# Retention attention and two MLPs on one core: plain products between the first attention units, four staging tiles, and weights moved between queues

## The chip, the cores and the metric

The kernel runs on one core of one Trainium2 chip. The metric is the device time of one execution in microseconds (us); lower is better. Three runs of the kernel before took 1064.4, 1069.26 and 1070.01 us, so its median is 1069.26 us.

The engines are TensorE (PE; its weight loads are shown apart as PEld), VectorE (DVE), ScalarE (ACT) and GpSimd (POOL). SyncE (SP) does no arithmetic here: it issues DMA transfers, and so does POOL. Each engine works through its own instructions in order.

## The reference, cut to what matters

An attention with a decaying state feeds a first MLP, which feeds a second.

```python
# q, k, v: (4 batches, 8 heads, 768 positions, 64)
gamma = 1.0 - 2.0 ** (-5.0 - np.arange(H))
for t in range(S):
    state = gamma * state + outer(k[:, :, t], v[:, :, t])
    y[:, :, t] = scale * einsum('bhd,bhde->bhe', q[:, :, t], state)
x = y.transpose(0, 2, 1, 3).reshape(3072, 512)

h = x @ w_in                      # first MLP: 512 -> 2048 -> 512
x = np.maximum(0.01 * h, h) @ w_out
h = np.maximum(x @ w_in2, 0.0)    # second MLP, weights of its own
return h * h @ w_out2
```

## The kernel before, in words

**Tiles.** The 3072 tokens are worked on in three blocks of 1024, each of two tiles of 512 tokens. A layer's 2048 inner columns are cut into 8 pairs (`NQ = 8`, the `q` of the code), each of two groups of 128 columns in each half. Weights are cast on the chip: ACT and DVE turn a piece into a high part and a low part (`scale_words`, `shift`, `sign`, `add`, then `high` and `low`), and a product is made of high x high, high x low and low x high, so a product of 128 columns is twelve matmuls of 128x512.

**Attention.** It is cut into 24 units. `attend` issues one: 64x64 matmuls `sc`, `y` and `inc` on PE, mask and state steps on DVE, copies on ACT. A unit is at most 120 matmuls and as many weight loads. The inputs `r` (queries, keys, values) come by loads on SP, `prep_to` prepares them. Units 0 to 7 stand in the head of the program, the others between the products of layer one. Inside layer one, `group()` issues a unit and the loads for the next units.

**Layer one, block one.** `emit_plain(q, i, t)` is a plain product (twelve matmuls) of pair q; `put_out` and `emit_out` are the products with the output weights, which add into the banks `acc`. In the head two plain products stand behind units 5 and 6. `begin_loop` ends the head, `plain_period(q)` runs for q = 1 to 7, and a second half of steps i = 0 to 15 puts out the other half, with a `group()` at i = 0, 2, 4, 6 and 8. From q = 4 on a period has a group as well.

**Layer one, block two.** `strassen_period(q)`, q = 0 to 7, uses seven products in place of eight. In the same stretch further weights are cast: `load_piece(n)` reads a 512 KB piece of the raw weights (`st<-w`) into a staging tile, `begin` casts it on ACT and DVE. Two staging tiles alternate (`t{NQ - 2 + n % 2}`).

**Later blocks.** `both_block(lay, b)` runs four times, first (0,2), then (1,0), (1,1) and (1,2), each with nine steps n: the first half of pair n and the second half of pair n - 1. In (1,0) the sums of the output weights of the second MLP that are still missing are made beside it: `make_units(q, f, ...)` reads a half of the weights (`of<-wflt`, on the POOL queue, since it goes by `store`) and adds up and casts quarters of it. Input weights of a pair come by `wa<-wid` and `wb<-wid` on the SP queue.

**What sets the order.** In `strict` stretches (the head, the periods) every instruction keeps the order in which the code issues it; elsewhere a scheduler orders them on each engine by the data they need. `mm` (L133) records every matmul, `load` (L136) issues a transfer on SP and `store` (L139) one on POOL, so most rows of a profile carry one of these lines, and the names of the tiles tell which step it is.

Of the kernel before, what the change touches and what calls it, by code (L numbers as in the profile page):

```python
# [47 lines left out]
MORE = 12  # L48
SOON = [(q, 0) for q in FIRST + (0, 1, 4, 6)] + [(q, 1) for q in range(NQ) if q not in HERE]
# [7 lines left out]
def retention_then_two_mlps(  # L57
# [251 lines left out]
    wou = [dram.tile([P, 8, NQ, 2, 256], F32, name=f"wou{lay}") for lay in range(2)]  # L309
# [257 lines left out]
    def sums_low(q):  # L567

        f = quarters_of(stage.pop(("of", q)))
        for n, (t, u) in enumerate(stage.pop(("u", q))):  # L570
            low(u[:, :, 1], f[:, 2 * n:2 * n + 2], u[:, :, 0])
            store(
                out=wou[0][:, 4 + 2 * n:6 + 2 * n, q].rearrange("p n l c -> p n (l c)"),
                in_=t.rearrange("p (n c) -> p n c", n=2),
            )
# [21 lines left out]
    def sum_units(lay, q, f, *to):  # L597
        sum_up(f)
        for n in range(2):
            out_units(lay, q, 4 + 2 * n, f[:, n * 512:n * 512 + 512].rearrange("p (n c) -> p n c", n=2), to[n])  # L600

    def all_units(q, f, *to):
# [3 lines left out]
        sum_units(1, q, f, *to[2:])  # L606
# [220 lines left out]
    def read_stage(lay, n, ks):  # L827
        i = STAGES[n]
        for k in ks:
            if n < 5:  # L830
                tag = (("xh1", "xl1", "xh5", "xl5"), ("xh6", "xl6", "xh3", "xl3"), ("xh7", "xl7", "xh2", "xl2"))[n % 3 if n < 3 else n - 2][k]
                t = x_p.tile([P, 2, 2, 256], F32R, tag=tag, name="wu")
            else:
                t = g_p.tile([P, 2, 2, 256], F32R, tag=f"t{4 * (n - 5) + k}", name="wu")
            load(out=t.bitcast(F32), in_=wou[lay][:, OUNIT[i], 2 * k:2 * k + 2])
            units[i, k] = t
# [79 lines left out]
    def both_block(lay, b, here):  # L916

        nl, nb = (lay, b + 1) if b + 1 < NB else (1, 0) if not lay else (None, None)
        pa = None
        for n in range(NQ + 1):  # L920
            f = first_half(lay, b, n) if n < NQ else iter(())
            r = second_half(lay, b, n - 1, pa) if n else iter(())
            if (lay, b) == (1, 0) and 3 <= n <= 6:
                with aside():
                    next(here[n // 5], None)
            if (lay, b) == (1, 0) and n == NQ - 1:
                with aside():
                    next(made, None)
            for k in range(4):
                pa = next(f, None)  # L930
                if n == NQ - 1 and k < 2:
                    read_stage(lay, 0, (2 * k, 2 * k + 1))
                if lay == 0 and n and (k == 1 or k == 3 and n in (1, 2, 4, 5)):
                    with aside():
                        next(here, None)
                if k < 3:
                    next(r, None)
            if n == NQ - 1:
                read_stage(lay, 1, range(4))
            if n and n + 1 < NQ and ((lay, b) != (1, 0) or n not in (3, 5)):  # L940
                read_units(lay, n + 1)
            if (lay, b) == (1, 0) and n < NQ - 1 and n != 5:
                if n == 0:
                    v = quarters() + scratch("ss", "ss", "wb", "wf")
                else:
                    with aside():
                        next(made, None)
                if n in (0, 2, 4):
                    made = make_units(5 + n // 2, *v[:5])
                    next(made)  # L950
                    if n == 0:
                        here = [units_here(4, v[5], v[7]), units_here(6, v[6], v[5])]
                        for m in here:
                            next(m)
# [77 lines left out]
    loads_to(1)  # L1032
    load_w(0, 0)
    load(out=tabs_t, in_=tabs)
    loads_to(NP)
    prep_to(1)
    h = [slice(0, 512), slice(512, 1024)]
    for n in range(ND):
# [4 lines left out]
        if n == 0:  # L1043
            s, f = open_in(0)
            for c in h:
                scale_words(s[:, c], f[:, c])
        elif n == 1:
            a = hold_in(0)
            for k in range(2):
                high(a[:, 0, 2 * k:2 * k + 2], quarters_of(f)[:, 2 * k:2 * k + 2])  # L1050
        if n == 0:
            prep_to(2)
# [5 lines left out]
        elif n == 1:  # L1058
            for k in range(2):
                o = slice(2 * k, 2 * k + 2)  # L1060
                low(a[:, 1, o], quarters_of(f)[:, o], a[:, 0, o])
        elif n == 4:
            load_w(1, 0)
            load_w(0, 1)
        if n == 6:
            first_in = open_in(1)
            scale_words(*first_in)
        if n in (5, 6):
            emit_plain(0, n - 5, 0)
        if n == 6:  # L1070
            shift(first_in[1])
            sign(*first_in)
# [4 lines left out]
    add(*first_in)  # L1077
# [29 lines left out]
    def begin_loop(first):  # L1107

        (w, f), out = first
        load_w(2, 0)  # L1110
        load_w(1, 1)
        load_w(2, 1)
        a = hold_in(1)
        high(a[:, 0], quarters_of(f))
        emit_plain(0, 0, 1)
        low(a[:, 1], quarters_of(f), a[:, 0])
        store(out=wraw[1], in_=f)
        emit_plain(0, 1, 1)
# [5 lines left out]
        for j in range(2):  # L1124
            split_high(j)
            split_rest(j)

    def plain_period(q):

        last = q == NQ - 1  # L1130
        early = q > 1

        load_w(q + 2, 0)
        if early:
            split_high(2 * q - 2)
# [5 lines left out]
        if not early:  # L1141
            o = hold_out(0)
            high_out(0, o)
        emit_plain(q, 0, 0)
        if early:
            split_rest(2 * q - 2)
            sums_high(q - 1)
        else:
            low_out(0, o)
# [4 lines left out]
        if early:  # L1154
            split_high(2 * q - 1)
        emit_plain(q, 1, 0)
        if early:
            split_rest(2 * q - 1)
            sums_low(q - 1)
# [18 lines left out]
        if not early:  # L1178
# [3 lines left out]
        for s, r in out:  # L1182
            add(s, r)
        if not early:
            sum_up(stage["of", 0])
        load_w(q + 2, 1)

        put_out(0, 2 * q - 2)
        if early and not last:
            a = hold_in(q + 1)  # L1190
            high(a[:, 0], quarters_of(f))
            low(a[:, 1], quarters_of(f), a[:, 0])
        if last:
# [3 lines left out]
        if not early:  # L1197
            sums_high(0)
        if q == 2:
            loads_to(ND + 1)  # L1200
            value_loads_to(ND + 1)
            loads_to(ND + 2)
        if q > 3:
# [5 lines left out]
        if not early:  # L1209
            sums_low(0)  # L1210
        if not last:
            sum_up(stage["of", q])
        if q >= 3:
            prep_to(n_score[0] + 1)
# [9 lines left out]
    def strassen_period(q):  # L1224
# [41 lines left out]
        load_piece(n + 1)  # L1266
# [13 lines left out]
        load_piece(n + 2)  # L1280
# [64 lines left out]
    for b in range(NB - 1):  # L1345
        strict[0] = True
        if b == 0:
            begin_loop((first_in, out0))
            for q in range(1, NQ):
# [25 lines left out]
        for i in range(NJ):  # L1375
# [6 lines left out]
            if b == 0 and i in (0, 2, 4, 6, 8):  # L1382
# [101 lines left out]
```

## Time and profile before

| | |
|---|---|
| median of three runs | 1069.26 us |
| the profiled execution, own time | 1072.81 us |
| its span, first to last instruction | 1071.0 us |
| PE busy | 1031.1 us (96%) |
| DVE busy | 763.6 us (71%) |
| ACT busy | 584.6 us (55%) |
| granted clock of PE, mean | 0.988 |
| moved by DMA | 294.01 MB, mean 275 GB/s |

The profiled execution lies 3.6 us above the median; 1.8 us of its time lie outside its span. PE is the engine to look at: where it stands still, the table of waits says what it waited for. The granted clock is a share of full speed (2.4 GHz); 0.50 is the lower of its two levels, 1.2 GHz. "issue" as a cause of a wait means that the engine waited for nothing that the profile shows.

### The profile page before, as it was taken

Reading aid. Unit: us, or ns where it says so; the run is one execution under the profiler, and the core shown is the slowest. Engines: PE = TensorE matmul, PEld = TensorE weight load, DVE = VectorE, ACT = ScalarE, POOL = GpSimd, SP = SyncE. Lnnn points to the kernel's source line nnn. Section 1 sums busy time; section 2 is a strip of 40 time slices with the busy share of each in tenths; the row PEclk is TensorE's granted clock in tenths of the full one; section 3 lists DMA queues with packets and bytes.
Section 4 is the critical chain, followed back from the end, with each engine's and each line's share of the span. In section 5 each row is a group of like instructions: output and inputs, shape, how many; then the busy total and the mean of one; then the engine's idle time right before and its main releaser. Section 6 shows DMA issues by size and latency. Waiting matters only on the chain.

```text
span 1071.0 us, 18364 instructions
## 1 busy us (share of the span) xinstructions
PE 1031.1 (96%) x7135; PEld 843.8 (79%) x7135; DVE 763.6 (71%) x1272; ACT 584.6 (55%) x996; POOL 91.6 (9%) x156
## 2 busy tenths in 40 slices
PE   5899999799898999999999998999999999999998
PEld 4678888687787788887788777888888888888886
DVE  5688878686687759487888767977555868356953
ACT  3566655445546447377566556655455555455542
POOL 0012111101000000122110111100000001000000
PEclk9999999999999999999999998999999999999999
DMA  8489967997999978889987487977256775367461
GB/s 306 164 326 376 325 254 236 404 329 260 361 389 342 357 251 296 331 308 393 355 286 314 155 306 273 404 254 287 86 200 223 298 270 201 128 206 258 171 239 59
DMA packets 81445, 294.01 MB, mean 275 GB/s; under 512 B 8400, under 2 KB 8656, under 8 KB 74704
## 3 DMA queue, kind: packets, MB, share of 16 engines
q1 hardware_dynamic: 61536, 212.56, 55.1%
q0 software_dynamic: 19680, 80.23, 19.2%
q8 instruction: 56, 0.92, 0.3%
q14 instruction: 29, 0.24, 0.1%
q10 hardware_dynamic: 144, 0.07, 0.0%
HBM read 206.84 MB, written 85.98 MB: 273 GB/s over the span
## 4 chain that ended last, share of the span: by engine, by line
PE 78%; DMA 14%; DVE 3%; ACT 2%; issue 2%; SPq 0%; POOL 0%; ACTq 0%; DVEq 0%; POOLq 0%
PE acc L133 42%; PE pa L133 21%; PE pd L133 8%; DMA st<-w 6%; DMA r<-first 4%; PE pb L133 4%; DMA of<-wflt 2%; PE y L133 2%; PE inc L133 1%; DMA wa<-wid 1%; PE sc L133 1%; DMA wraw<-wf 1%; SPq L136 0%; DMA wid<-wa 0%; ACT gh L732 0%
## 5 line engine op out<-in xcount | busy, mean ns | idle before, releaser
L133 PE MATMUL acc<-rot,wu 128*128 128x512 f32 x1344 | 308.3, 391 | 0.0
L133 PEld LDWEIGHTS acc<-rot,wu 128*128 128x128 f32 x1344 | 252.4, 188 | 55.3
L133 PE MATMUL pa<-xh,wa 128*128 128x512 f32 x576 | 179.9, 394 | 3.3 <-ACT g L721 1.4
L841 DVE TENSOR_TENSOR rot<-gu,rot 128x512 fp32r<-128x512 f32 x160 | 109.4, 689 | 46.4 <-ACT rot L840 45.5
L840 ACT CAST rot<-gu 128x512 fp32r<-128x512 f32 x160 | 99.4, 621 | 77.2 <-PE acc L133 53.6
L133 PEld LDWEIGHTS pa<-xh,wa 128*128 128x128 f32 x576 | 107.7, 189 | 29.1 <-DMA wa<-wid 3.0
L133 PE MATMUL acc<-gh,wo 128*128 128x512 f32 x400 | 106.0, 398 | 7.0 <-ACT gh L732 7.0
L133 PE MATMUL pa<-xl,wa 128*128 128x512 f32 x288 | 112.7, 391 | 0.0
L133 PE MATMUL pd<-xh,wa 128*128 128x512 f32 x320 | 99.7, 393 | 2.7 <-ACT gt L862 2.7
L133 PE MATMUL pa<-xh,wb 128*128 128x512 f32 x320 | 100.3, 395 | 0.5 <-DVE gt L875 0.5
L133 PEld LDWEIGHTS acc<-gh,wo 128*128 128x128 f32 x400 | 75.2, 190 | 24.9 <-ACT gh L732 8.3
L133 PEld LDWEIGHTS pd<-xh,wa 128*128 128x128 f32 x320 | 60.4, 189 | 15.8 <-ACT gt L862 3.1
L133 PEld LDWEIGHTS pa<-xh,wb 128*128 128x128 f32 x320 | 59.6, 189 | 14.0 <-DVE gt L875 1.4
L841 DVE TENSOR_TENSOR rot<-gt,rot 128x512 fp32r<-128x512 f32 x64 | 44.1, 691 | 29.4 <-ACT rot L840 29.0
L133 PEld LDWEIGHTS pa<-xl,wa 128*128 128x128 f32 x288 | 54.3, 189 | 11.6
L133 PE MATMUL pd<-xl,wa 128*128 128x512 f32 x160 | 62.7, 392 | 0.0
L133 PE MATMUL pa<-xl,wb 128*128 128x512 f32 x160 | 62.3, 390 | 0.0
L840 ACT CAST rot<-gt 128x512 fp32r<-128x512 f32 x64 | 39.8, 622 | 38.7 <-DVE rot L841 27.0
L133 PE MATMUL acc<-gl,wo 128*128 128x512 f32 x200 | 57.0, 393 | 0.0
L712 ACT ACTIVATE gt<-gt 128x512 f32<-128x512 f32 x48 | 30.4, 632 | 46.6 <-DVE gt L868 33.8
L880 DVE TENSOR_TENSOR gu<-gu,pb 128x512 f32<-128x512 f32 x32 | 22.0, 687 | 43.7 <-PE pb L133 43.7
L737 DVE TENSOR_TENSOR gl<-g,gh 128x512 fp32r<-128x512 f32 x50 | 34.2, 689 | 23.4 <-ACT gh L732 18.8
(133 smaller groups left out, 1691.5 us busy)
## 6 DMA issues: line engine op xcount, KB each, us to landing
wu<-wou SPq DMA_DIRECT2D x112, 512.0 KB, 6.0
wa<-wid SPq DMA_DIRECT2D x28, 1024.0 KB, 7.6
wou<-of POOLq DMA_DIRECT2D x48, 512.0 KB, 7.0
wb<-wid SPq DMA_DIRECT2D x28, 768.0 KB, 5.1
wo<-wou SPq DMA_DIRECT2D x20, 1024.0 KB, 8.5
r<-first SPq DMA_DIRECT2D x64, 256.0 KB, 8.2
st<-w SPq DMA_DIRECT2D x24, 512.0 KB, 9.4
wid<-wa POOLq DMA_DIRECT2D x12, 1024.0 KB, 9.3
```

What stands on the lines that cost most here:

```text
L133: pin(nc.tensor.matmul(**kw))
L712: nc.scalar.activation(out=g, in_=g, func=AF.Relu)
L737: mark[1] = seq(nc.vector.tensor_tensor(out=gl, in0=g, in1=gh.bitcast(F32), op=ALU.subtract)).ins
L840: mark[0] = nc.scalar.copy(r[:, 0], s).ins
L841: mark[1] = nc.vector.tensor_tensor(out=r[:, 1], in0=s, in1=r[:, 0].bitcast(F32), op=ALU.subtract).ins
L880: nc.vector.tensor_tensor(out=u[:, 0], in0=u[:, 0], in1=pb, op=ALU.add)
```

## The change

It has five parts. (1) In the head four plain products, not two, stand behind units 4 to 7, one behind each; inputs are read in another order, the weights of pairs 0 and 1 are cast earlier, and `begin_loop` takes over what the period q = 1 did. (2) Period q = 3 has an attention group too, and the second half has groups at i = 0, 2, 5 and 8. (3) Four staging tiles hold raw pieces in block two, and pieces are read up to a period earlier. (4) A pair's output weights of layer one go to an own tensor `wpl`, 8 KB in a row per partition, in place of four rows of 2 KB; the reads of units 0 to 3 in the third block take two rows of 2 KB where they took one of 4 KB. (5) In block (1,0) the first read of `make_units` moves from the POOL queue to the SP queue, ahead of the loop over n, and its steps are spread over more places.

```diff
+STAGED = (6, 7, 4, 5, 6, 7, 4, 5, 6, 7, 6, 7)
...
-                t = g_p.tile([P, 512], U64, tag=f"t{NQ - 2 + n % 2}", name="st", bufs=1)
+                t = g_p.tile([P, 512], U64, tag=f"t{STAGED[n - EARLY]}", name="st", bufs=1)
             load(out=t, in_=w2[q, half][:, c])
...
         store(
-            out=wou[0][:, 0:4, q].rearrange("p n l c -> p n (l c)"),
-            in_=o.bitcast(F32).rearrange("p n l c -> p n (l c)"),
+            out=wpl[:, q], in_=o.bitcast(F32).rearrange("p n l c -> p (n l c)"),
         )
...
-    def make_units(q, f, *to):
-
-        store(out=f, in_=wflt[q, 1])
-        yield
-        yield from all_units(q, f, *to)
+    def make_units(q, f, *to, put=store, apart=False):
+
+        put(out=f, in_=wflt[q, 1])
+        yield
+        yield from all_units(q, f, *to, apart=apart)
...
         load(
-            out=t.bitcast(F32).rearrange("p n l c -> p n (l c)"),
-            in_=wou[0][:, 0:4, q].rearrange("p n l c -> p n (l c)"),
+            out=t.bitcast(F32).rearrange("p n l c -> p (n l c)"), in_=wpl[:, q],
         )
...
+        here_too = (lay, b) == (1, 0)
+        if here_too:
+            v = quarters() + scratch("ss", "ss", "wb", "wf")
+            made = make_units(5, *v[:5], put=load, apart=True)
+            next(made)
         for n in range(NQ + 1):
...
+                if here_too and (n, k) in ((2, 0), (4, 0), (4, 2), (6, 0)):
+                    with aside():
+                        next(made, None)
...
     loads_to(1)
+    load(out=tabs_t, in_=tabs)
+    loads_to(3)
     load_w(0, 0)
-    load(out=tabs_t, in_=tabs)
-    loads_to(NP)
+    loads_to(4)
...
     for n in range(ND):
-        attend(True, (lambda: prep_to(min(n_score[0] + 1, ND))) if n else None)
-        if n < 2:
-            busy(3 - n)
+        attend(True, ahead_of(n) if n else None)
+        if n == 0:
+            busy(3)
+            prep_to(2)
         loads_to(min(n + 4, ND))
...
         elif n == 4:
-            load_w(1, 0)
             load_w(0, 1)
-        if n == 6:
-            first_in = open_in(1)
-            scale_words(*first_in)
-        if n in (5, 6):
-            emit_plain(0, n - 5, 0)
-        if n == 6:
-            shift(first_in[1])
-            sign(*first_in)
+            emit_plain(0, 0, 0)
+            s, f = open_in(1)
+            for c in h:
+                scale_words(s[:, c], f[:, c])
+        elif n == 5:
+            emit_plain(0, 1, 0)
+            shift(f)
+            sign(s, f)
+            add(s, f)
+            a = hold_in(1)
+            for k in range(2):
+                o = slice(2 * k, 2 * k + 2)
+                high(a[:, 0, o], quarters_of(f)[:, o])
+                low(a[:, 1, o], quarters_of(f)[:, o], a[:, 0, o])
+            store(out=wraw[1], in_=f)
+            load_w(2, 0)
+        elif n == 6:
+            emit_plain(1, 0, 0)
+            split_both(0)
+        elif n == 7:
+            split_both(1)
+            emit_plain(1, 1, 0)
...
-        if q > 3:
+        if q > 2:
             group()
...
-        load_piece(n + 1)
+        for k in {0: (n + 2, n + 3), 4: (), 5: (n + 1,)}.get(q, (n + 3,)):
+            load_piece(k)
...
-        load_piece(n + 2)
+        if q != 3:
+            load_piece(n + 4 if q < 3 else n + 2)
...
-            if b == 0 and i in (0, 2, 4, 6, 8):
+            if b == 0 and i in (0, 2, 5, 8):
                 group()
...
                 load_piece(EARLY)
+                load_piece(EARLY + 1)
```

The order of the instructions moves at three places that matter below. On PE, in the head, before: `inc` ends an attention unit, `pa` is a plain product with `xh`, `xl` as its tokens and `wa` as its weights, and `sc` begins the next unit.

```order
L133 MATMUL inc_544<-r_380 64x64 x4
L133 MATMUL pa_618<-xh1_287,wa_301 128x512 x2
...
L133 MATMUL pa_618<-xl5_451,wa_301 128x512
L133 MATMUL sc_633<-r_458 64x64 x2
...
L133 MATMUL inc_634<-r_459 64x64 x4
L133 MATMUL pa_709<-xh1_287,wa_301 128x512 x2
...
L133 MATMUL sc_726<-r_535 64x64 x2
...
L133 MATMUL y_803<-r_535,pm_789 64x64 x12
L133 MATMUL pa_857<-xh6_610,wa_301 128x512 x2
```

And the same place now:

```order
L134 MATMUL inc_464<-r_285 64x64 x4
L134 MATMUL pa_542<-xh1_276,wa_379 128x512 x2
...
L134 MATMUL sc_562<-r_366 64x64 x2
...
L134 MATMUL inc_563<-r_367 64x64 x4
L134 MATMUL pa_637<-xh1_276,wa_379 128x512 x2
...
L134 MATMUL inc_664<-r_458 64x64 x4
L134 MATMUL pa_736<-xh1_276,wa_655 128x512 x2
...
L134 MATMUL inc_756<-r_537 64x64 x4
L134 MATMUL pa_833<-xh1_276,wa_655 128x512 x2
```

One product stands one unit earlier than the first did, and two products of the second pair's weights (`wa_655`) follow the next units where before none of that pair stood between units.

On SP, at the start of block two, before: `st` is a raw piece for the staging tiles, `wf` a read of weights cast before, `wo` a pair's output weights, `r` attention inputs.

```order
L136 DMA wf_2906<-wflt2_0_104 128x512
L136 DMA st_2908<-w2 128x512
L136 DMA wo_2955<-wou0_121 128x4x512
L136 DMA st_3022<-w2 128x512
L136 DMA wf_3045<-wraw2_103 128x1024
L136 DMA wflt7_0_119<-xs_2991 128x512
L136 DMA st_3051<-w2 128x512
L136 DMA r_3131<-first 128x512
```

And now:

```order
L137 DMA wf_2909<-wflt2_0_104 128x512
L137 DMA st_2911<-w2 128x512
L137 DMA st_2913<-w2 128x512
L137 DMA wo_2960<-wpl_123 128x2048
L137 DMA st_3027<-w2 128x512
L137 DMA st_3029<-w2 128x512
L137 DMA wf_3052<-wraw2_103 128x1024
L137 DMA wflt7_0_119<-xs_2996 128x512
L137 DMA st_3058<-w2 128x512
L137 DMA r_3138<-first 128x512
```

Two more pieces are issued ahead of the first attention inputs, and each piece stands ahead of work that it stood behind.

On SP, in block (1,0), before: `wa` and `wb` are a pair's input weights, `wu` output weights.

```order
L136 DMA wu_6213<-wou0_121 128x1024
L136 DMA wu_6215<-wou0_121 128x1024
L136 DMA wa_6470<-wid1_2_91 128x2048
L136 DMA wb_6471<-wid1_2_91 128x1536
L136 DMA wa_6545<-wid1_3_92 128x2048
```

And now, with `of`, the half of pair 5's output weights that `make_units` adds up:

```order
L137 DMA wu_6216<-wpl_123 128x2x512
L137 DMA wu_6218<-wpl_123 128x2x512
L137 DMA of_6367<-wflt5_1_114 128x1024
L137 DMA wa_6473<-wid1_2_91 128x2048
L137 DMA wb_6474<-wid1_2_91 128x1536
L137 DMA wa_6552<-wid1_3_92 128x2048
```

The read of 512 KB now stands on SP directly ahead of the weights of pair 2; before it stood on POOL, behind six stores of `ydr`.

## Rows read from the trace of the kernel before

**Rows 1.** PE on the page: busy us, share of the span, instructions.
```profile
PE 1031.1 (96%) x7135; PEld 843.8 (79%) x7135; DVE 763.6 (71%) x1272; ACT 584.6 (55%) x996; POOL 91.6 (9%) x156
```

**Rows 2.** PE's waits, 0 to 63 us (waited for: us, times, longest us).
```profile
PE y L133 <- issue: 10.7, 6, 4.4
...
PE sc L133 <- DMA r<-first: 1.4, 1, 1.4
```

**Rows 3.** PE's waits, 63 to 176 us.
```profile
PE pa L133 <- ACT g L721: 1.4, 1, 1.4
```

**Rows 4.** The instruction queue in the page's list (packets, MB, share).
```profile
q8 instruction: 56, 0.92, 0.3%
```

**Rows 5.** Chain that ended last, 0 to 75 us (start us, us, what).
```profile
19.42 4.42 issue
...
30.34 2.80 issue
...
34.60 2.94 PE pa L133 x12
...
38.28 1.27 issue
...
44.35 1.22 DVE wf L376
```

**Rows 6.** PE's waits, 176 to 250 us.
```profile
PE inc L133 <- DMA r<-first: 3.6, 1, 3.6
```

**Rows 7.** Chain that ended last, 190 to 225 us.
```profile
198.84 11.87 DMA r<-first
```

**Rows 8.** Three stretches: busy of PE, PEld, DVE, ACT, POOL; PEclk, DMA share, GB/s.
```profile
209.30:216.20 6.90, 5.35 (x72) 4.58 (x73) 3.15 (x5) 3.83 (x6) 0.00 (x0) 0.51 1.01 374
325.40:328.80 3.40, 3.40 (x10) 2.62 (x9) 2.49 (x6) 3.40 (x8) 0.00 (x0) 0.50 1.02 367
646.20:653.10 6.90, 6.21 (x15) 4.86 (x16) 6.18 (x13) 3.85 (x9) 1.99 (x3) 0.51 0.91 358
```

**Rows 9.** PE's waits, 250 to 386 us.
```profile
PE acc L133 <- ACT gh L732: 7.0, 3, 3.8
```

**Rows 10.** Chain that ended last, 250 to 386 us.
```profile
268.47 15.00 DMA st<-w
```

**Rows 11.** SP's transfers in order of time, 264 to 287 us.
```profile
272.69 0.32 SPq L136 DMA_DIRECT2D wf<-wraw  x1
```

**Rows 12.** The tile `wraw` alone, 250 to 386 us.
```profile
DMA to landing us min/median/max: 4.1/10.3/12.5
```

**Rows 13.** Two stretches, columns as in Rows 8.
```profile
140.00:180.00 40.00, 40.00 (x414) 33.05 (x413) 32.30 (x59) 21.51 (x36) 4.89 (x7) 1.00 0.59 208
...
260.00:320.00 60.00, 56.76 (x577) 46.05 (x576) 46.98 (x99) 33.16 (x66) 3.17 (x6) 1.00 1.00 373
```

**Rows 14.** DMA, 250 to 386 us.
```profile
DMA packets 15984, 46.03 MB, mean 338 GB/s; under 512 B 1489, under 2 KB 1489, under 8 KB 15074
```

**Rows 15.** PE's waits, 580 to 660 us.
```profile
PE pd L133 <- ACT gt L862: 2.7, 1, 2.7
PE pa L133 <- DMA wa<-wid: 0.8, 1, 0.8
PE pa L133 <- ACT gu L859: 0.7, 1, 0.7
```

**Rows 16.** Chain that ended last, 600 to 660 us.
```profile
608.30 15.54 DMA of<-wflt
```

**Rows 17.** SP's transfers in order of time, 600 to 616 us.
```profile
604.97 0.32 SPq L136 DMA_DIRECT2D wa<-wid  x1
```

**Rows 18.** DMA issues, 600 to 660 us (count, KB each, median us to landing).
```profile
wa<-wid SPq DMA_DIRECT2D x3, 1024.0 KB, 10.2
```

**Rows 19.** DMA issues of the whole span, from the page.
```profile
wa<-wid SPq DMA_DIRECT2D x28, 1024.0 KB, 7.6
...
wo<-wou SPq DMA_DIRECT2D x20, 1024.0 KB, 8.5
```

More of the change, by code (lines that the diff above doesn't have):

```diff
@@ L595, in sum_up, with all_units @@
         tt(out=a12, in0=a12, in1=a22, op=ALU.subtract)
[L597 to L602, printed above, removed]
+    def all_units(q, f, *to, apart=False):
         for n in range(2):
@@ L937, in both_block @@
                     next(r, None)
+                if here_too and (n, k) in ((2, 0), (4, 0), (4, 2), (6, 0)):
+                    with aside():
+                        next(made, None)
             if n == NQ - 1:
                 read_stage(lay, 1, range(4))
-            if n and n + 1 < NQ and ((lay, b) != (1, 0) or n not in (3, 5)):
+            if n and n + 1 < NQ and (not here_too or n not in (3, 5)):
                 read_units(lay, n + 1)
[L942 to L945, printed above, removed]
+            if here_too:
+                if n in (1, 2, 4, 6):
                     with aside():
                         next(made, None)
-                if n in (0, 2, 4):
-                    made = make_units(5 + n // 2, *v[:5])
+                if n == 0:
+                    here = [units_here(4, v[5], v[7]), units_here(6, v[6], v[5])]
+                    for m in here:
+                        next(m)
+                elif n in (2, 4):
+                    made = make_units(5 + n // 2, *v[:5], apart=True)
                     next(made)
[L951 to L954, printed above, removed]
         A = [ps["acc"].tile([P, T], F32, tag=f"acc{m}", name="acc") for m in range(2)]
@@ L1046, in retention_then_two_mlps @@
                 scale_words(s[:, c], f[:, c])
[L1047 to L1052, printed above, removed]
+        elif n == 2:
+            load_w(1, 0)
             for c in h:
@@ L1076, in retention_then_two_mlps @@
     scale_words(*out0[1])
-    add(*first_in)
     start.close()
@@ L1105, in group, with begin_loop @@
         loads_to(n + 2)
-    def begin_loop(first):
-        (w, f), out = first
-        load_w(2, 0)
+    def begin_loop(out):
+        emit_plain(0, 0, 1)
         load_w(1, 1)
         load_w(2, 1)
[L1113 to L1118, printed above, removed]
+        w, f = open_in(2)
+        scale_words(w, f)
         for s, r in out:
@@ L1123, in begin_loop @@
             add(s, r)
-        for j in range(2):
-            split_high(j)
-            split_rest(j)
+        emit_plain(0, 1, 1)
+        shift(f)
+        sign(w, f)
+        add(w, f)
+        store(out=wraw[2], in_=f)
+        load_w(3, 0)
+        o = hold_out(0)
+        high_out(0, o)
+        low_out(0, o)
+        emit_plain(1, 0, 1)
+        out = open_out(1)
+        for s, r in out:
+            scale_words(s, r)
+        sum_up(stage["of", 0])
+        emit_plain(1, 1, 1)
+        a = hold_in(2)
+        high(a[:, 0], quarters_of(f))
+        for s, r in out:
+            shift(r)
+            sign(s, r)
+        low(a[:, 1], quarters_of(f), a[:, 0])
+        for s, r in out:
+            add(s, r)
+        load_w(3, 1)
+        loads_to(ND + 1)
+        value_loads_to(ND + 1)
+        loads_to(ND + 2)
+        put_out(0, 0)
+        sums_high(0)
+        o = hold_out(1)
+        high_out(1, o)
+        sums_low(0)
+        low_out(1, o)
+        sum_up(stage["of", 1])
+        put_out(0, 1)
     def plain_period(q):
         last = q == NQ - 1
-        early = q > 1
         load_w(q + 2, 0)
-        if early:
-            split_high(2 * q - 2)
+        split_high(2 * q - 2)
         if not last:
@@ L1140, in plain_period @@
             load_in(0)
-        if not early:
-            o = hold_out(0)
-            high_out(0, o)
         emit_plain(q, 0, 0)
[L1145 to L1149, printed above, removed]
+        split_rest(2 * q - 2)
+        sums_high(q - 1)
         if not last:
@@ L1177, in plain_period @@
             next(made)
-        if not early:
+        for s, r in out:
+            add(s, r)
+        load_w(q + 2, 1)
+        put_out(0, 2 * q - 2)
+        if not last:
             a = hold_in(q + 1)
@@ L1181, in plain_period @@
             low(a[:, 1], quarters_of(f), a[:, 0])
[L1182 to L1193, printed above, removed]
+        else:
             next(made)
@@ L1208, in plain_period @@
             split_rest(NJ - 2)
-        if not early:
-            sums_low(0)
-        if not last:
+        else:
             sum_up(stage["of", q])
-        if q >= 3:
-            prep_to(n_score[0] + 1)
+        prep_to(n_score[0] + 1)
         if not last:
@@ L1347, in retention_then_two_mlps @@
         if b == 0:
-            begin_loop((first_in, out0))
-            for q in range(1, NQ):
+            begin_loop(out0)
+            for q in range(2, NQ):
                 made = plain_period(q)
```

50 lines of the change are left out of this document (31 added, 19 removed).

## The prediction

> **What bounds the kernel now.** I began with the page. TensorE (PE) is busy for 96% of the span [rows 1], so only the time in which it stands still, and the time in which it runs at half clock, can be won. I then took the table of PE's waits in stretches that follow the stages, the chain that ended last inside each stretch with a large wait, and the granted clock right behind such a wait. Five places matter.
>
> In the head PE waits 10.7 us for "issue", and 1.4 for a transfer [rows 2]. The queue that carries instructions has 56 packets with 0.92 MB [rows 4], 16 KB each. PE executes 7135 matmuls [rows 1] and as many weight loads, so a packet holds about 255 instructions. An attention unit is at most 120 matmuls with their loads, about 240 instructions: nearly one packet for 2 us of work. I read the "issue" waits as waits for the next packet, between the units that follow each other without other work; 2.80 and 1.27 us of them stand at 30.34 and 38.28 us, the largest, 4.42 us, at 19.42 us [rows 5]. From 63 to 176 us there is one wait of 1.4 us [rows 3]. From 176 to 250 us a group waits 3.6 us for the transfer of its values [rows 6]. From 250 to 386 us three waits of 7.0 us in sum end with ACT's high part `gh` [rows 9]; the chain shows behind one of them a raw piece that took 15.00 us to land [rows 10]. In block (1,0) waits of 2.7 and 0.7 us end with ACT, and one of 0.8 us with `wa<-wid` [rows 15]; the chain shows behind ACT a read `of<-wflt` of 15.54 us [rows 16].
>
> Three of these waits are followed by a stretch at a granted clock of 0.50 to 0.51, the lower level [rows 8]. Work at half clock takes twice its time, so half of PE's busy time there is lost: 5.35 x 0.49 = 2.6 us, 3.40 x 0.50 = 1.7 us and 6.21 x 0.49 = 3.0 us.
>
> **The change part by part.** The sum is made against the profiled execution, 1072.81 us, which is 3.55 us above the median of 1069.26 us.
>
> *Head.* Two more plain products move up, so each of units 4 to 7 has a product of twelve matmuls behind it, which takes 2.94 us [rows 5] for 24 instructions. A packet then lasts about 2 + 2.94 us, and the two waits of 2.80 and 1.27 us go: -4.1 us. The 4.42 us stay, since no product stands there. Pair 0's weights are cast earlier, so I let the 1.4 us behind them go as well [rows 3]: -1.4. Against this stand new waits. A product right behind a unit needs its tokens' low part, and the third product needs the weights of pair 1. The cast is a chain of DVE steps of up to 1.22 us [rows 5]. With the first product alone a wait is between 0 and one such step, and I take 1.0. For pair 1 three such steps at most follow each other, so 0 to 3.7 us; I take half of it, 1.8. Head: -5.5 + 2.8 = -2.7 us, with ends of -5.5 (both hidden) and +4.9 us (both at their upper end, and the supply of instructions no better). That inputs land in another order I cost at nothing: only 1.4 us wait for them [rows 2]; nor do I count the two idle matmuls that go behind unit 1, since the next packet is awaited there.
>
> Instruction supply is the reading on which this rests. The Trainium skill, page "Runtime: NRT & Kernel Launch", section "Instruction fetch mechanics", has blocks of 16 KiB with 256 instructions, which fits the packets here, but calls the cost of crossing a block "mostly hidden". By that rule the 4.1 us would not come back, the head would cost +1.4 us, and the sum below would be -8.1; the trace disagrees so far, with 10.7 us of waits that no data explains.
>
> *Group in period three, and at 5 in place of 4 and 6.* The group that waits 3.6 us has its values' transfer issued at 198.84 us; it takes 11.87 us and lands at 210.71 [rows 7]. Moved behind one more output step of twelve matmuls, some 2.9 us like the product above, the group needs them 2.9 us later: 3.6 - 2.9 = 0.7 us are left, and I take 1.0, since the queue before it changes a little. The half clock behind it goes with a wait that short: -2.6. Together -2.6 - 2.6 = -5.2 us. The unit in period three is covered by a stretch that has hardly a wait; its transfers find room, for the DMA engines are at 0.59 from 140 to 180 us [rows 13]. Ends: -6.2 (no wait left) and +1 us (the transfer lands as much later as the group does, and 1 us is lost in period three).
>
> *Four staging tiles.* What goes is the wait for pieces: 7.0 us [rows 9] and 1.7 us of half clock, 8.7 in all. What is late next is the read `wf<-wraw`: one is issued at 272.69 us, behind the piece of 268.47 us [rows 10, 11], and such reads take up to 12.5 us [rows 12], so it lands within 2 us of that piece at 283.47. It too is issued earlier now, since it follows the cast of a piece. But the DMA engines are full there: 1.00 busy at 373 GB/s from 260 to 320 us [rows 13]. The stage moves 46.03 MB in 136 us [rows 14]; in 127.3 us, with the whole 8.7 saved, that is 362 GB/s, close below what the full stretch shows. Between 0 and 8.7 I take the middle, -4.3 us. It costs something too that two more pieces of 512 KB stand ahead of the first attention inputs; 1 MB at 373 GB/s is 2.8 us of later landing, hidden as long as inputs are issued a unit ahead, as they are.
>
> *A pair's output weights in one row.* No wait of PE names `wo` or `wu`. A read of 1024 KB from rows of 2 KB lands in 8.5 us, one from rows of 8 KB (`wa`) in 7.6 us [rows 19]; so 0 to 0.9 us per read, hidden behind a whole period. The units in the third block that are now read in halves of a row could cost as much. Taken as 0.
>
> *Block (1,0).* Out go the waits on ACT, 2.7 + 0.7 us [rows 15], and 3.0 us of half clock, as `of<-wflt` no longer stands behind six stores. In comes a later `wa`. Before, its read is issued at 604.97 us [rows 17], takes about 10.2 us [rows 18], lands at 615.2, and PE waits 0.8 us for it. Now 0.5 MB stands ahead of it on its queue and itself waits for a DVE step of about 1.2 us: 1.2 + 0.5/0.373 = 2.5 us later if the queue had all the engines, and 1.2 + 2.7 = 3.9 us if it shares them equally with POOL's transfers. I take 3.2 us, so PE waits 4.0, and behind a wait of that length the clock falls, for 2.6 to 3.0 us as in the rows at 209 and 646 us. Removed 7.2, added 4.0 + 3.0 = 7.0 (the 0.8 is in both): about 0. Ends: -6.4 (the wait for `wa` stays 0.8) and +4 (the next pair's read is late as well).
>
> Sum: -2.7 - 5.2 - 4.3 - 0 + 0 = -12.2 us. The profiled execution would come to 1060.6 us and the median to 1057.
>
> **The rivals.**
>
> *The head returns nothing.* The "issue" waits have a cause that products between units don't touch, or the waits for freshly cast weights take their place. For it: four products stand on work that DVE and ACT have just ended. Against it: one wait in all among the products and casts of the 113 us that follow [rows 3]. Time: 1069.3 - 8.1 = 1061 us.
>
> *Waits pass on.* The reads `wf<-wraw` are as late as the pieces were and the 4.3 us of the staging tiles come to nothing, and `wa` costs 3 us more. For it: a full DMA between 260 and 320 us. Time: 1057 + 4.3 + 3 = 1064 us.
>
> *More is won.* Pieces and casts run early enough, and `wa` lands in time: 1057 - 4.3 - 5 = 1048 us. The Trainium skill, page "Perfetto Trace Analysis", section "DMA Optimizations", says that going from 2 KB to 4 or 8 KB can improve throughput dramatically. If so, the full stretch would empty and all 8.7 us would come back; the two rows on reads of 1024 KB here differ by 0.9 of 8.5 us, which does not bear it out, so I give this case little.
>
> *Slower: the transfers set the time.* From 180 to 360 us the DMA engines have no room, so that what PE wins in the head or at a group it loses at the next transfer: the landing times stay, and head, groups and pieces return nothing. The two pieces that are read ahead then delay the first inputs by 2.8 us on the path, and in block (1,0) the read ahead of `wa` costs 4. Time: 1069.3 + 6.8 = 1076 us. For it: shares of 1.01, 1.02 and 1.00 in three rows [rows 8, 13]. Against it: 0.59 from 140 to 180 us, where an earlier start can catch up. It decides if that stretch fills up to about 0.98.
>
> **How the numbers follow.** Chances: forecast 0.42, head without gain 0.11, waits pass on 0.25, more won 0.09, slower 0.13. A measurement of this kernel can tell 0.5%, 5.3 us, from no change: faster is below 1063.9, slower above 1074.6. Faster: nearly all of the first two and of "more won", and half of "pass on": 0.40 + 0.10 + 0.09 + 0.12 = 0.71. Slower: 0.11 of the last. Same: 0.18. The forecast's own range is 1051 to 1062. The range goes up over "pass on" to 1068 and down to 1047, half into "more won"; it leaves out the slower case and some 0.05 on the low side.
>
> **What would show it.** In the changed profile: "issue" waits of PE before 63 us near 6.6 us; in the stretch with the half's groups no wait over 1.5 us for `r<-first` and a clock near 1.00; `gh` on ACT as a cause of PE's waits in block two at 0 to 4 us, and `st<-w` no longer in its chain; near 615 us a wait for `wa<-wid` of 3 to 5 us with half clock behind it, and none for ACT. The prediction is wrong if "issue" stays at 10 us or more, if the share from 140 to 180 us goes to 0.95 while PE's waits for transfers grow, or if `wa` lands in time.

## The result, and the profile after

The changed kernel takes 1061.19 us (median of 10 runs, 1053.3 to 1065.23), the kernel before on the same occasions 1069.62 us (10 runs, 1064.4 to 1075.96): a ratio of 0.9916, 95% interval 0.9891 to 0.994, that is 6.4 to 11.7 us less. A second set gave 1059.3 us and 0.9902 (0.9875 to 0.9929). The forecast was 1057 us, 12.2 us less, with a range of 1047 to 1068.

The profiled execution took 1057.65 us, 15.2 us less than the one of before. That is more than the medians differ, since one profile lies 3.5 us below its median and the other 3.2 us above; so one pair of profiles says less on a stage than several do, and the stages are counted over all kernels further down.

The first line of the page, busy us of each engine; it answers to [rows 1]:

```profile
PE 1026.1 (97%) x7133; PEld 842.1 (80%) x7133; DVE 764.4 (72%) x1273; ACT 586.0 (56%) x999; POOL 89.9 (9%) x155
```

PE has 5 us less busy time for the same matmuls but two. Either profile has four stretches at a granted clock of 0.50 in which PE works, one of them (before) or two (after) in the head; PE's busy time in them fell from 19.3 to 14.4 us. Half of that fall, 2.4 us, is time that half clock no longer costs; what the other 2.6 us are, these rows don't show. PE's waits by stage, with the stretches moved along with the work. The head, 0 to 60 us, beside [rows 2]:

```profile
PE sc L134 <- issue: 6.2, 3, 2.9
PE y L134 <- issue: 2.2, 2, 1.6
...
PE pa L134 <- ACT wa L393: 0.3, 1, 0.3
PE pa L134 <- DVE wa L396: 0.2, 1, 0.2
```

"issue" still takes 8.4 us of 10.7, but freshly cast weights cost 0.5 us and not 2.8. From 60 to 170 us, beside [rows 3], and from 170 to 244 us, beside [rows 6]:

```profile
PE pa L134 <- ACT g L720: 2.6, 1, 2.6
```

```profile
PE y L134 <- DVE xs L276: 3.7, 1, 3.7
```

The group's wait for its values is gone. From 60 to 170 us there is again one wait, at another place (before 95.1 us, in period two) and 1.2 us longer, and the group at i = 2 waits 3.7 us for DVE, where it waited 1.9 us in the kernel before (176 to 250 us):

```profile
PE y L133 <- DVE xs L275: 1.9, 1, 1.9
```

The chain of 185 to 202 us after the change shows why it grew:

```profile
179.97 15.97 DMA st<-w
...
195.96 0.68 ACT sf L369
...
199.41 0.60 DVE sf L384
200.01 0.61 DVE xs L276
```

A raw piece of the weights takes 15.97 us to land. Its cast stands ahead of the attention's `xs` on DVE; DVE is the engine that the wait names, but the chain leads back to the transfer. Block two, 244 to 378 us, beside [rows 9], and the full stretch in it, beside [rows 13]:

```profile
PE pa L134 <- ACT g L704: 1.0, 1, 1.0
```

```profile
254.00:314.00 60.00, 59.07 (x588) 47.98 (x588) 51.09 (x107) 36.65 (x73) 3.50 (x7) 1.00 1.02 391
```

All 7.0 us of waits for `gh` are gone in this profile and `st<-w` is no longer in the chain of this stretch. The full stretch moves 391 GB/s, where it moved 373. Block (1,0), 572 to 652 us, beside [rows 15], with the chain and the transfers of SP there, beside [rows 16 to 18]:

```profile
PE pa L134 <- DMA wa<-wid: 3.8, 1, 3.8
```

```profile
592.55 1.05 PE pa L134 x5
593.61 12.18 DMA wa<-wid
...
605.83 4.40 PE pa L134 x12
...
612.95 2.72 PE pa L134 x12
```

```profile
593.17 0.33 SPq L137 DMA_DIRECT2D of<-wflt  x1
593.61 1.30 SPq L137 DMA_DIRECT2D wa<-wid  x1
```

The waits on ACT are gone and `wa` is late by 3.8 us; the product that waited takes 4.40 us, a later one of the same size 2.72. The stretches at half clock, beside [rows 8]:

```profile
199.20:206.00 6.80, 5.34 (x128) 4.93 (x129) 6.01 (x13) 2.34 (x5) 0.00 (x0) 0.50 1.05 422
605.40:608.80 3.40, 2.97 (x7) 2.39 (x8) 2.80 (x6) 1.27 (x3) 0.00 (x0) 0.50 1.03 428
```

The one in block two is gone; that of the groups has stayed, now behind the wait for DVE; that in block (1,0) is half as long.

### The profile page after: what moved, and what is told of

It is laid out like the page before. It is cut to its first block, busy times and chain, and to the rows that moved or that the text cites. A ratio compares the mean times of both kernels' runs of the same rounds, so it can differ in the third digit from the quotient of the medians.

```text
span 1055.6 us, 18359 instructions
## 1 busy us (share of the span) xinstructions
PE 1026.1 (97%) x7133; PEld 842.1 (80%) x7133; DVE 764.4 (72%) x1273; ACT 586.0 (56%) x999; POOL 89.9 (9%) x155
## 3 DMA queue, kind: packets, MB, share of 16 engines
q0 software_dynamic: 18512, 79.70, 19.3%
## 4 chain that ended last, share of the span: by engine, by line
PE 84%; DMA 10%; DVE 3%; ACT 1%; SPq 1%; issue 1%; ACTq 0%; DVEq 0%
PE acc L134 43%; PE pa L134 25%; PE pd L134 9%; PE pb L134 5%; DMA wa<-wid 2%; DMA wf<-wraw 2%; DMA r<-first 2%; DMA st<-w 2%; DMA sg<-w 1%; PE y L134 1%; PE sc L134 1%; SPq L137 1%; DMA wo<-wpl 1%; PE inc L134 1%; DVE wa L396 0%
## 5 line engine op out<-in xcount | busy, mean ns | idle before, releaser
L134 PE MATMUL pb<-xh,wb 128*128 128x512 f32 x160 | 49.5, 391 | 0.8 <-DVE pm L256 0.8
```

Of the source, the lines that this page charges most:

```text
L134: pin(nc.tensor.matmul(**kw))
```

## The experiments

Each of the five parts was made alone on the kernel before, parts were put together or one was taken out, and two other places were tried. Ratios are to the kernel before, run on the same chip; a range behind a ratio is its 95% interval.

**The head alone.** The head's edits of the diff on the kernel before, `begin_loop` with them; the groups stay at their places:

```diff
         elif n == 4:
-            load_w(1, 0)
             load_w(0, 1)
...
+            emit_plain(0, 0, 0)
...
+            emit_plain(0, 1, 0)
...
+            emit_plain(1, 0, 0)
...
+            emit_plain(1, 1, 0)
...
-    def begin_loop(first):
...
+    def begin_loop(out):
```

> Only the head of the change, on the kernel before: four plain products behind units 4 to 7, casts and inputs earlier; groups, staging tiles, rows and block (1,0) as before. Theory: products between units cover the supply of instructions, so the work up to the end of the first 24 matmuls of acc ends about 4.4 us earlier (68.0 against 72.4 us), and a wait for a freshly read weight piece near 92 us does not appear, since that one comes from the group in period three: about 1065 us, 4 us less than before. Rival 1: the head's 4 us are taken back near 92 us by the same transfers, with or without the group: a wait of 2.6 us there, about 1067 us. Rival 2: the head gives nothing by itself: 1069 us, issue waits before 63 us still at 10 us.

1068.75 us, 0.9994 (0.997 to 1.0017): rival 2 in the median, but not in its reason. "Issue" waits before 63 us fell to 8.6 us, and the head ends 3 us earlier; at the end of block one 0.6 us of this is left in this pair of profiles (237.8 against 238.4 us). PE's waits from 176 to 250 us, and the chain:

```profile
PE inc L133 <- DMA r<-first: 5.2, 1, 5.2
PE y L133 <- DVE xs L275: 0.5, 1, 0.5
```

```profile
196.77 13.18 DMA r<-first
```

The values' transfer is issued 2.07 us earlier than in [rows 7], but takes 13.18 us and not 11.87, and lands only 0.8 us earlier. PE waits 5.2 us for it, not 3.6, but for DVE 0.5 us and not 1.9, so both waits together are 5.7 us where they were 5.5. That the head's gain is given back at this transfer is therefore not shown: the kernel with the four staging tiles alone, which has the old head, also waits 5.2 us for `r<-first` there, and the profile of the head alone is 2.8 us faster than its median. The interval of the ratio leaves room for a gain of up to 3.2 us.

**The groups alone.**

```diff
-        if q == 2:
+        if q == 1:
             loads_to(ND + 1)
...
-        if q > 3:
+        if q > 2:
             group()
...
-            if b == 0 and i in (0, 2, 4, 6, 8):
+            if b == 0 and i in (0, 2, 5, 8):
```

> Only the attention group in period three and the groups at i = 0, 2, 5, 8, on the kernel before; the inputs of the first groups are read one period earlier for it. Theory: the wait of 3.6 us for the values' transfer goes, but the group's transfers in period three delay a weight piece (a wait of about 2.6 us near 95 to 105 us), the wait for DVE at i = 2 grows from 1.9 to about 3.7 us as the piece before it lands later, and the half clock behind it stays: no gain, 1069 to 1070 us. Rival: the two new waits come from the earlier start of everything, not from the group; then this kernel has neither, and gains the 5.2 us that were forecast: 1064 us.

1072.7 us, 1.0025 (1.0002 to 1.0048): as the theory, a little worse. The wait in the periods, 60 to 176 us, its chain, and the clock behind it:

```profile
PE pa L133 <- ACT g L721: 5.9, 2, 4.3
```

```profile
82.47 14.77 DMA wraw<-wf
...
98.33 1.13 ACT sg L368
```

```profile
98.90:105.70 6.80, 5.71 (x13) 4.46 (x14) 5.62 (x9) 6.04 (x12) 1.98 (x3) 0.50 0.34 133
```

A store of cast weights takes 14.77 us; ACT waits for it ahead of the next piece, and PE for ACT, 4.3 us, and then runs at half clock (5.71 x 0.50 = 2.9 us). The waits for values at the later groups fell from 3.6 to 2.4 us. The group of period three begins at 99 to 108 us in the profiles that have it, and that stretch was fuller in the kernel before than the one of [rows 13]:

```profile
60.00:140.00 80.00, 78.64 (x519) 64.58 (x518) 65.99 (x100) 55.59 (x84) 13.61 (x20) 1.00 0.93 345
```

**The four staging tiles alone.**

```diff
+STAGED = (6, 7, 4, 5, 6, 7, 4, 5, 6, 7, 6, 7)
...
-        load_piece(n + 1)
+        for k in {0: (n + 2, n + 3), 4: (), 5: (n + 1,)}.get(q, (n + 3,)):
+            load_piece(k)
...
-        load_piece(n + 2)
+        if q != 3:
+            load_piece(n + 4 if q < 3 else n + 2)
...
```

> Only the four staging tiles with their earlier reads, on the kernel before. Theory: all waits for pieces in block two go, with the half clock behind the longest: 8 to 9 us less, 1061 us, with no wait over 1.2 us of PE between 250 and 386 us. Rival 1: half of it was won only with the pair's output weights in one row, which makes the transfers of this stretch cheaper; then waits for the reads of weights cast before remain, 4 us less, 1065 us. Rival 2: the gain came from the group that moved out of the stretch before: nothing, 1069 us.

1062.08 us, 0.9922 (0.9898 to 0.9947): the theory in its median, 7.4 us less. Of the three waits for `gh` one of 1.7 us is left, where the theory allowed 1.2, and no stretch at half clock. PE's waits from 245 to 384 us:

```profile
PE acc L134 <- ACT gh L733: 1.7, 1, 1.7
PE pa L134 <- ACT g L706: 1.0, 2, 0.7
```

**Block (1,0) alone.**

```diff
...
+            made = make_units(5, *v[:5], put=load, apart=True)
+            next(made)
         for n in range(NQ + 1):
...
```

> Only the change in block (1,0): the first read of a half of the output weights on SP ahead of the loop, the steps spread. Theory: waits on ACT of 3.4 us and 3.0 us of half clock go; a wait of about 3.8 us for the input weights of pair 2 comes with some 1.7 us of half clock in place of 0.8: 2 to 3 us less, 1067 us. Rival: the wait for the input weights and the clock behind it eat all of it, 1069 us or more; or the wait came from the earlier part of the kernel being ahead, then it is under 1 us here and 6 us are won, 1063 us.

1071.98 us, 1.0027 (0.9998 to 1.0055): the first rival. One wait in place of three, from 590 to 665 us:

```profile
PE pa L133 <- DMA wa<-wid: 3.9, 1, 3.9
```

**The rows alone.**

```diff
-            out=wou[0][:, 0:4, q].rearrange("p n l c -> p n (l c)"),
+            out=wpl[:, q], in_=o.bitcast(F32).rearrange("p n l c -> p (n l c)"),
...
```

> Only the fourth part of the change on the kernel before: a pair's output weights in one row of 8 KB, the reads of units 0 to 3 of the third block in two rows of 2 KB. Theory: no wait of PE hangs on these transfers, and those they share the queue with gain under 1 us: 1069 to 1070 us. Rival 1: the whole change without this part was 3 us faster than with it, so by itself it costs 3: 1072 to 1073 us. Rival 2: fewer packets ease the full stretch from 180 to 360 us, 1067 us or less.

1067.69 us, 0.9977 (0.9952 to 1.0002): between the theory and rival 2, and against rival 1. Block two keeps its waits for `gh`, 6.5 us.

**The whole change again.** The kernel after the change, without an edit.

> The whole change once more, beside the kernel before and beside the three kernels of this set: how far two profiles of one kernel differ. Theory: the median is again 1060 to 1062 us, but the profile differs from the first by several us, in the places of half clock and in the waits for transfers between 60 and 240 us; the wait for pair 2's input weights in block (1,0) is there again, 3 to 4 us. Rival: the first profile is typical, stage by stage within 1 us.

1059.3 us (6 runs), a little under the theory. The wait for `wa` is there again, 3.5 us, but with twice the half clock behind it, and the stages differ from those of the first profile by up to 3.2 us. PE's waits from 572 to 652 us, and the stretch behind:

```profile
PE pa L134 <- DMA wa<-wid: 3.5, 1, 3.5
```

```profile
604.30:611.10 6.80, 5.38 (x13) 4.23 (x14) 3.83 (x8) 1.85 (x3) 1.47 (x3) 0.50 1.02 422
```

**The whole change without the rows.**

```diff
-            out=wpl[:, q], in_=o.bitcast(F32).rearrange("p n l c -> p (n l c)"),
+            out=wou[0][:, 0:4, q].rearrange("p n l c -> p n (l c)"),
...
```

> The whole change without its fourth part: the pair's output weights stay in four rows of 2 KB. Theory: transfers between 60 and 386 us set the time wherever something waits, and 8 KB rows take some of their load off; without them 1 to 3 us come back as waits, 1062 to 1064 us, with waits for pieces or `gh` of 1 to 3 us in block two. Rival 1: the rows are nothing, 1061 us and no wait for `gh` in block two. Rival 2: they carry half of the gain in block two: 1066 us.

1056.01 us, 0.9871 (0.9847 to 0.9895), beside 1059.3 with the rows: rival 1 as to the waits (0.8 us for `gh` in block two). The two tries on the rows have opposite signs (2.0 us less with them above, 3.3 us more here), and the pair of kernels further down that differ in the rows alone has 0.9872 and 0.9871. So the rows are not told from nothing.

**Head, staging tiles and rows.** The head as above, without the groups and with block (1,0) as before.

> Head, staging tiles and rows of the change; the groups at their old places and block (1,0) as before. Theory: the groups' new places and block (1,0) cost about what they win or 2 us more, so this is 1058 to 1061 us, with a wait of 3 to 5 us for a group's values near 205 us and no wait over 1 us near 95 us. Rival: the groups are needed, since the head's gain is lost at the group near 205 us without them: 1063 to 1065 us.

1059.51 us, 0.99 (0.987 to 0.9929): the median of the theory, though not with the waits it names: there is one of 1.9 us near 95 us, and at the groups, from 176 to 250 us, DVE is waited for longer than the values:

```profile
PE y L134 <- DVE xs L276: 3.7, 2, 3.3
PE inc L134 <- DMA r<-first: 1.6, 1, 1.6
```

The kernel before waits 5.5 us at these groups, this one 5.3. The rival, 1063 us or more without the groups, did not come.

**Head and groups.** Both edits together, the rest as before.

> Head and groups of the change together on the kernel before, the rest as before. Theory: the head alone gave under 1 us and the groups alone lost 3, because each leaves the wait at the other's place; together the head's 3 us pass the group at 205 us, which no longer waits long for its values: the second half of block one ends near 233.5 us (before 238 to 243), and the median is 1062 to 1064 us. Rival: the two singles add up, 1070 to 1072 us, and the second half ends at 237 us or later.

1061.52 us, 0.9933 (0.9912 to 0.9955): the theory, and against the sum of the singles. Block one ends at 230.7 us, where the theory had 233.5. PE's waits from 60 to 176 us, then from 176 to 250 us:

```profile
PE pa L133 <- ACT g L721: 1.6, 1, 1.6
```

```profile
PE y L133 <- DVE xs L275: 2.1, 1, 2.1
PE inc L133 <- DMA r<-first: 0.2, 1, 0.2
```

**The read behind the input weights.** The whole change, but:

```diff
-            next(made)
         for n in range(NQ + 1):
...
-                if here_too and (n, k) in ((2, 0), (4, 0), (4, 2), (6, 0)):
+                if here_too and (n, k) in ((2, 0), (2, 2), (4, 0), (4, 2), (6, 0)):
...
             if here_too:
-                if n in (1, 2, 4, 6):
+                if n == 1:
+                    next(made)
+                if n in (2, 4, 6):
```

> The whole change, but the first read of a half of the output weights stands on SP behind the input weights of pair 2, and its first steps come half a step of the loop later. Theory: the wait of 3.8 us for the input weights and the half clock behind it (1.7 us) go, and the read, no longer behind POOL's stores, lands in time for ACT: 3 to 5 us less than the whole change, 1056 to 1058 us. Rival: the wait passes on to ACT (`of` lands at 622 us or later, as before the change), and half of it comes back: 1060 us.

1057.24 us, 0.9872 (0.9843 to 0.9901); the whole change on the same chip had 1059.3. The median is as the theory has it, but 2 us less than the whole change, where the theory had 3 to 5. From 572 to 652 us:

```profile
PE pa L134 <- DMA wa<-wid: 1.6, 2, 1.0
```

**The best of both.** The last kernel without the rows.

> Whole change without the rows, and with the read of the output weights behind the input weights of pair 2 in block (1,0). Theory: the better place of the read is worth about 2.5 us and the rows nothing or a loss: 1054 to 1056 us, the least of all kernels here; against the same kernel with the rows (1057.2 us) 0 to 3 us less. Rival: the three us by which the kernel without rows was below the whole change were scatter, and this is 1057 us.

1056.1 us, 0.9871 (0.9848 to 0.9894): one of the two lowest medians, no better than the one without the rows alone. It can't be told from the last kernel (1057.2).

**Groups at i = 0, 3, 6, 8.**

```diff
-            if b == 0 and i in (0, 2, 5, 8):
+            if b == 0 and i in (0, 3, 6, 8):
```

> As the kernel before in this set, with the groups of the second half at i = 0, 3, 6, 8. Theory: the wait of about 3 us for DVE near 197 us comes from a raw piece that lands at 196 us and not from the group itself; with the group one step later its tokens stand ahead of the next piece's cast on DVE, and the wait goes: 2 us less than with 0, 2, 5, 8. Rival: the wait is taken over by the output product of that step, which needs the same DVE engine, or the later groups wait for their transfers: same time.

1058.36 us, 0.989 (0.9865 to 0.9915): the rival. The wait near 197 us, which is 1.5 us in the last kernel and not the 3 of the theory, is gone, and from 170 to 244 us there are two others, one for a transfer that stood behind no wait before:

```profile
PE acc L134 <- DMA wo<-wou: 3.1, 1, 3.1
PE y L134 <- DVE xs L276: 1.8, 1, 1.8
```

**The stages over all profiles.** The program's end of a stage is taken at the same matmul in each trace: the 24th, the 336th and the 552nd that writes `acc`, and the 480th and last that writes `pd`, 85 us before the end of the span (some records can be missing, worth a few tenths). In us, of one profile for each kernel: the head, the rest of block one, block two to the start of the third block, and from there through block (1,0) to that last `pd`.

| kernel | head | block one | block two | rest |
|---|---|---|---|---|
| before | 72.4 | 166.0 | 156.1 | 591.7 |
| head alone | 69.4 | 168.4 | 155.7 | 586.0 |
| groups alone | 71.2 | 168.4 | 154.8 | 588.3 |
| head and groups | 67.5 | 163.2 | 154.1 | 587.5 |
| staging tiles alone | 73.9 | 166.1 | 149.2 | 587.3 |
| rows alone | 72.2 | 167.5 | 155.7 | 588.0 |
| block (1,0) alone | 71.9 | 171.5 | 153.8 | 589.0 |
| whole change | 68.0 | 166.7 | 147.0 | 589.2 |
| whole change again | 67.4 | 164.1 | 150.2 | 590.2 |
| without the rows | 69.6 | 163.3 | 148.5 | 589.2 |
| head, tiles and rows | 70.3 | 168.3 | 148.0 | 588.5 |
| read behind `wa` | 69.1 | 165.8 | 148.4 | 586.7 |
| read behind `wa`, without the rows | 70.0 | 165.4 | 147.6 | 586.4 |
| the same, groups at 0, 3, 6, 8 | 67.4 | 169.3 | 151.3 | 587.5 |

## Why the prediction was right, and where its terms were off

The direction and the range held; of the forecast gain of 12.2 us the medians show 8.4 and 10.6 us. The signs against the prediction stayed away: "issue" waits fell below 10 us, the DMA share from 140 to 180 us is 0.57 (0.59 before), and `wa` was late. By means over the table, the five kernels with the old head against the nine with the new, and so on, the parts are:

- *Head:* forecast -2.7, measured 68.75 - 72.32 = -3.6 us. The reading of "issue" as a wait for the next packet of instructions was right. The traces hold the times of the DMA packets: in the kernel before, instruction packets of 16 KB had landed at 15.89, 22.61, 31.72 and 38.21 us, and PE went on at 17.15, 23.84, 33.15 and 39.55 us. All 51 waits for "issue" over 0.5 us before 63 us, in all 14 profiles, end 1.2 to 1.6 us after such a packet has landed. But the term was too large, -4.1 us: 8.4 of 10.7 us remain, as means 7.3 of 8.9. In units 5 and 6, where 2.80 and 1.27 us were to go, 0.7 and 0.6 us are left, while unit 4, which no product precedes, now waits 1.6 us; units 2 and 3, which no product covers, have 2.6 and 2.9 where they had 1.7 and 4.4. The price for freshly cast weights was too high, 2.8 against 0.5 (1.3 as a mean, up to 2.0). And the inputs, set at nothing, gave as much as "issue": the waits for `r` and its preparation fell from 2.6 to 0.7 us as means. The wait of [rows 3] went from its place, but one of 0.8 to 3.1 us at 92 to 95 us came in the period after, in all nine kernels with the new head; three of the five with the old one have a wait of 1.0 to 2.6 us near 115 us that none of the nine has.
- *Groups:* forecast -5.2. With the head, the six kernels with groups at 0, 2, 5 and 8 have 164.75 us in block one, the four with the old head and old groups 167.76: -3.0 (the two with the new head and old groups have 168.35, which would make it -3.6). The step that the values would arrive in time was right in four of the six profiles (3.6 us to 0.2 or nothing); in the two others 2.5 and 3.0 us of waits for them stay. The step that the half clock would go was wrong in the first profile: it hung on a wait of 3.7 us for DVE, behind a late raw piece, which was 1.9 us before and which the prediction doesn't name. And period three was not free: the share of 0.59 was that of the stretch from 140 us on, while the group begins at 99 to 108 us, in a stretch with 0.93 (60 to 140 us, before).
- *Head and groups as terms to add:* this step was wrong. Alone they have ratios of 0.9994 and 1.0025, each known to within 0.0024; together 0.9933. The ends of block one say the same: 240.4 us as a mean of the four kernels with neither, 238.2 with the new head and the old groups (two), 239.6 with the new groups and the old head (one), 233.4 with both (six). Why is argued and not shown. The rival "the transfers set the time" fits a part of each: in the kernel with the head alone a start that comes 2.07 us earlier is a landing 0.8 us earlier, and the groups alone meet a wait of 4.3 us near 100 us, with 2.9 us lost to half clock behind it. With both, the moved group needs its values later, and the wait near 95 us is 1.1 to 2.6 us.
- *Staging tiles:* forecast -4.3, the middle between two ends; measured 148.77 - 155.03 = -6.3 us; alone, by medians, 5.7 to 10.9 us. The waits for `gh` are 5.9 to 7.0 us in all six profiles with two tiles and 0 to 2.5 us in all eight with four. The reads `wf<-wraw` that were to be late next did come into the chain (10.63 and 11.41 us there), but they don't take longer: from 244 to 378 us their median to landing is 8.9 us, where it was 10.3, and PE waits only 1.0 us. The full stretch had room: 391 GB/s and not 373 (373 to 397 in the eight profiles with four tiles, 345 to 374 in the six with two). The rate that a stretch full of waits showed was no ceiling here.
- *Rows:* forecast 0; not told from 0 in three comparisons. The page "Perfetto Trace Analysis" of the Trainium skill, section "DMA Optimizations", says that going from 2 KB to 4 or 8 KB can improve throughput dramatically. The traces don't agree as to block two: the rows alone leave its 6.5 us of waits for `gh`, and the whole change without them has it as short as with them (148.5 us). A read of 1024 KB lands in 7.9 us and not 8.5.
- *Block (1,0):* forecast 0 with `wa` 4.0 us late; `wa` is 3.5 to 4.0 us late in all four profiles with that order. Measured 589.4 - 588.2 = +1.2 us. What was off is the price of what went: 7.2 us in the profile of before, but in the six other profiles with the old order PE waits 0 to 1.8 us for ACT's `gt` and not 2.7, and none has half clock there; without those 3.0 us the forecast would have been +3. One profile was taken for the typical one. With the read behind `wa` the three profiles have 586.9 us as a mean, 2.5 us less than with the read ahead of it.

The parts sum to -3.6 - 3.0 - 6.3 + 1.2 = -11.7 us, the medians to 8.4 and 10.6, with intervals that just reach it (6.4 to 11.7 and 7.6 to 13.4). That this sum lies 0.5 us from the forecast is luck: the terms were off by -0.9, +2.2, -2.0 and +1.2 us, and these cancel. Where the rest between sum and medians is I leave open: profiles scatter by 3.5 us about the median, and no stage shows a loss of that size.

By the rule in "Runtime: NRT & Kernel Launch", section "Instruction fetch mechanics", of the Trainium skill, which calls the cost of crossing a block "mostly hidden", the waits for "issue" would not have moved. They did move with the order of PE's instructions, from ahead of `y` to ahead of `sc`, and fell by 2.3 us (1.6 as means), and each ended behind the landing of an instruction packet, as told above; so in this head that cost is not hidden. Why the packets come so late no run here shows.

## What to carry to other kernels

Don't add gains on the two sides of a stretch that transfers fill as if they were separate: here an earlier start alone and a later need alone gave nothing that could be measured as a gain, and both together 0.7%. So try both ends of such a stretch together before you drop either. Put a new read behind the transfer that PE needs next, not ahead of it; 0.5 MB ahead of 1 MB made PE wait 3.5 to 4.0 us here in four profiles, against 0.6 to 1.9 us in the ten with another order. Before a term is taken from a wait, ask whether a second profile of the same stage has it. And a forecast that comes out right as a sum still has to be read term by term.

## What the runs showed that was not expected

The same wait is followed by half clock of different length: in the whole change 3.8 us for `wa` by 3.4 us at 0.50, 3.5 us by 6.8 us when it was run again. And the time lost to it is not tied to the longest waits: 2.50 us before the change, ahead of 285.99 us, had none behind it, a wait of 1.9 us near 95 us in the kernel with the read behind `wa` had 3.4 us. So the clock adds 0 to 3 us to a wait of this size, and a forecast should carry that as a range.
